# The refinement of the reciprocal rms moved from VectorE to GpSimd, and another order of the attention's events

## The chip, the cores and the metric

One core of a Trainium2 chip runs the whole kernel. Its engines work side by side, each through its own list of instructions in order: PE (TensorE, matrix products; PEld is its weight load), DVE (VectorE), ACT (ScalarE), POOL (GpSimd) and SP (SyncE, which here issues the DMA requests). The metric is the device time of one launch in microseconds (us); lower is better.

## What is computed

The reference, cut to what matters: attention with a normalisation by the root of the mean square on q and k, then a soft mixture of experts, then a two-layer network.

```
def rmsnorm(x, g):
    rms = np.sqrt(np.mean(x * x, axis=-1, keepdims=True) + 1e-06)
    return x / rms * g
# q, k, v: 4 batches, 12 heads, 448 rows, 64 columns
q_n, k_n = (rmsnorm(q, g_q), rmsnorm(k, g_k))
scores = q_n @ k_n.T / 8
attn = np.exp(scores - max) / (sum + 1e-9)
attn_out = attn @ v                       # 1792 x 768 over all heads
# soft mixture of 8 experts, 4 slots each, w1 768 x 1024, w2 1024 x 768
logits = x @ phi;  d = softmax over rows;  c = softmax over slots
slot_out = relu((d.T @ x) @ w1) @ w2;  x = c @ slot_out
# network, w_in 768 x 2048, w_out 2048 x 768
h = x @ w_in;  g = max(h, 0) + alpha * min(h, 0);  out = g @ w_out
```

## The kernel before

**Tiling.** The attention runs over 24 pairs of heads (4 batches times 6). Two pairs are one group for loading and for the normalisation, so there are 12 groups; pairs 2g and 2g+1 belong to group g. The 896 rows of a pair (two heads of 448) are cut into seven chunks of 128 rows. For every pair and chunk there is a product for the row maximum (`rowmax_mm`, PE; `rowmax`, VectorE), a score product (`score_mm`, PE), two exponentials (`score`, ACT), the difference between the f32 and the f16 exponential (`score_lo`, on GpSimd for chunks 3 and 6, on VectorE for others, on none for two) and a product with v (`av`, PE). After the attention the expert weights stream through (lines 1285 and 1314), and then the network runs (lines 1392 to 1521).

**The normalisation.** For each pair ACT squares q and k (line 641) and VectorE sums the squares into `u` (line 643), 28 columns for a group: two tensors, two pairs, seven chunks. `norm_rs` then makes `y`, the reciprocal of the rms: ACT takes Ln and Exp (lines 653 and 654), and one Newton step refines the result, y * (1.5 - u' * y * y) with u' half the mean square and the epsilon (lines 656 to 663). GpSimd multiplies q by y, k by the gains and then by y (`split_mul`, line 684), ACT casts to f16 (line 690), GpSimd subtracts to get the low part (`split_lo`, line 697), and PE transposes both (line 710). ACT copies the result out of PSUM (line 717), and SP issues small copies inside SBUF: `turned` (lines 719 and 721) and `twin`, which copies q to the other half of the partitions (line 726).

**The order.** Nothing of the attention is scheduled while it runs: the instructions of every engine are issued in the order in which the program was written out. The program first collects 2374 events in a list `plan`, always the same way (lines 1084 to 1140), and then sorts it by a tuple of literal positions, `ORDER`:

```
        assert sorted(ORDER) == list(range(len(plan)))
        plan = [plan[i] for i in ORDER]
```

`norm_rs` is cut into five events by its `yield`s: Ln and Exp; the scaling of `u`; nothing; y * y; the last two instructions. GpSimd's queue holds `split_mul`, `split_lo`, its `score_lo`, a little of the experts' sums, and it executes them in that order. SP's queue holds every request in the same way; a request that waits holds up those behind it. Weight loads are events of this list too, first in small pieces (`adv_pf`); when the last pair's scores are done, `close_score` frees buffers and all the loads that fit are issued in one go.

Of the kernel before, what the change touches and what calls it, by code (L numbers as in the profile page):

```python
# [16 lines left out]
ALU = mybir.AluOpType  # L17
# [336 lines left out]
def fused_attention_softmoe_mlp(  # L354
# [292 lines left out]
    def norm_rs(g):  # L647
# [5 lines left out]
        nc.scalar.activation(y, u, AF.Ln, scale=1.0 / D, bias=eps)  # L653
        nc.scalar.activation(y, y, AF.Exp, scale=-0.5)
        yield
        nc.vector.tensor_scalar(out=u, in0=u, scalar1=-0.5 / D, scalar2=-0.5e-6, op0=ALU.mult, op1=ALU.add)
        yield
        yield
        nc.vector.tensor_mul(t, y, y)
# [891 lines left out]
```

## Time and profile before

| | us |
|---|---|
| median of 3 runs | 698.97 |
| lowest and highest run | 695.72, 707.88 |
| the profiled execution | 698.2 |
| its span in the trace | 696.2 |

The span is the time from the first to the last recorded instruction. Busy times are sums over an engine's instructions; the chain that ended last is followed back from the last instruction, at each step to what released it. An engine's idle time is put down to the event that ended it. Times on GpSimd are rougher than on the other engines.

### The profile page before, as it was taken

The page shows a single profiled execution, that of the slowest core. Times are in us where ns is not written, and L with a number is a line of the kernel's source. Part 1 is how long each engine was busy: PE and PEld are TensorE (multiplying, and loading weights), DVE is VectorE, ACT ScalarE, POOL GpSimd, SP SyncE. Part 2 cuts the span into 40 slices and gives each one's busy share as a digit, 9 for nine tenths or more (in the row PEclk, how much of TensorE's full clock was granted, in tenths as well). Part 3 has the DMA queues.
Part 4 walks back from the last instruction along what each step waited for, and adds up shares of the span by engine and source line. Part 5 has one row for each costly group of instructions (what it writes and reads, how often), then busy time and mean ns, then how long its engine had stood idle before and what let it go on. Part 6 is the DMA issues. An engine that isn't in the chain of part 4 may idle for free.

```text
span 696.2 us, 14030 instructions
## 1 busy us (share of the span) xinstructions
PE 618.2 (89%) x5522; PEld 479.6 (69%) x5522; DVE 472.7 (68%) x967; ACT 364.5 (52%) x708; POOL 192.6 (28%) x200
## 2 busy tenths in 40 slices
PE   0799898898889999998998657899999999999997
PEld 0367665576656766775543213787899999999997
DVE  5788997899999999864311042999975545454541
ACT  2799996898898997772111121766531111111110
POOL 5976665466647654321101000000000000000000
PEclk9889999999999999998899979999999999999999
DMA  5477666644735622759799999250020101010101
GB/s 138 109 209 197 174 161 190 178 118 115 191 93 154 180 50 61 211 164 399 313 422 425 425 423 425 107 182 1 1 91 0 47 1 46 1 45 1 47 1 45
DMA packets 65425, 106.90 MB, mean 154 GB/s; under 512 B 34632, under 2 KB 51536, under 8 KB 61008
## 3 DMA queue, kind: packets, MB, share of 16 engines
q1 hardware_dynamic: 65360, 106.01, 45.6%
q8 instruction: 43, 0.70, 0.4%
q14 instruction: 22, 0.18, 0.1%
HBM read 92.18 MB, written 5.51 MB: 140 GB/s over the span
## 4 chain that ended last, share of the span: by engine, by line
PE 50%; DVE 23%; DMA 12%; ACT 8%; issue 3%; SPq 2%; POOL 2%; ACTq 0%; DVEq 0%; POOLq 0%
PE psa L1461 9%; PE psa L1460 9%; PE psa L1459 9%; DMA unit<-in_moe_w_dram 8%; DVE m L769 4%; PE psn L778 4%; PE psv L837 3%; PE psv L827 3%; PE psa L1285 2%; DVE e L810 2%; PE psr L760 2%; DVE wf L510 1%; ACT e L794 1%; PE psa L1314 1%; PE pst L1416 1%
## 5 line engine op out<-in xcount | busy, mean ns | idle before, releaser
L1459 PE MATMUL psa<-whi,gh 128*128 128x384 f32 (+1 forms) x448 | 152.7, 341 | 0.0
L1460 PE MATMUL psa<-wlo,gh 128*128 128x384 f32 (+1 forms) x448 | 151.8, 339 | 0.0
L1461 PE MATMUL psa<-whi,gl 128*128 128x384 f32 (+1 forms) x448 | 151.4, 338 | 0.0
L769 DVE TENSOR_REDUCE m<-psr 128x1 f16<-128x448 f32 x168 | 97.2, 615 | 5.9 <-PE psr L760 5.4
L1428 ACT CAST gh<-t 128x512 fp32r<-128x512 f32 x40 | 24.9, 622 | 123.0 <-DVE t L1425 122.5
L1461 PEld LDWEIGHTS psa<-whi,gl 128*128 128x128 f32 x448 | 84.7, 189 | 3.0 <-DVE gl L1408 0.2
L1460 PEld LDWEIGHTS psa<-wlo,gh 128*128 128x128 f32 x448 | 84.7, 189 | 2.8
L837 PE MATMUL psv<-vH,e 128*128 128x65 f16 (+1 forms) x1152 | 85.7, 195 | 1.0 <-DVE e L810 0.9
L1459 PEld LDWEIGHTS psa<-whi,gh 128*128 128x128 f32 x448 | 84.7, 189 | 2.6
L837 PEld LDWEIGHTS <-e 128*128 128x128 f16 (+1 forms) x1728 | 80.8, 106 | 1.5 <-DVE e L810 1.2
L1422 DVE TENSOR_SCALAR t<-pst,alpha_t 128x256 f32<-128x256 f32 x80 | 34.9, 476 | 61.9 <-PE pst L1416 61.9
L810 POOL TENSOR_TENSOR e<-ef,e 128x448 f16<-128x448 f32 x48 | 53.7, 1119 | 83.1 <-ACT ef L799 65.4
L827 PEld LDWEIGHTS psv<-vR,e 128*128 128x128 f32 (+1 forms) x384 | 59.6, 178 | 22.9 <-issue 10.9
L837 PE MATMUL psv<-vL,e 128*128 128x64 f16 (+1 forms) x576 | 73.7, 193 | 0.1
L794 ACT ACTIVATE e<-psn 128x448 f16<-128x448 f32 x120 | 65.1, 542 | 14.2 <-PE psn L778 11.1
L778 PE MATMUL psn<-q,k 128*128 128x448 f16 (+1 forms) x192 | 62.5, 368 | 11.0 <-DVE e L810 4.9
L827 PE MATMUL psv<-vR,e 128*128 128x65 f32 (+1 forms) x384 | 69.9, 264 | 1.9 <-DVE X L865 0.7
L760 PE MATMUL psr<-k,q 128*128 128x448 f16 (+1 forms) x192 | 58.8, 378 | 6.8 <-DVE m L769 4.0
L778 PE MATMUL psn<-qB,kB 67*128 67x448 f16 (+1 forms) x192 | 62.2, 364 | 2.8 <-DMA vR<-in_v_dram 2.8
L697 POOL TENSOR_TENSOR sp<-nf,sp 128x448 f16<-128x448 f32 x48 | 51.2, 1076 | 13.9 <-ACT sp L690 11.0
L810 DVE TENSOR_TENSOR e<-psn,e 128x448 f16<-128x448 f32 x72 | 44.2, 616 | 9.3 <-ACT psn L799 8.8
L710 PE MATMUL pst<-ident,sp 128*128 128x128 f16 x336 | 28.4, 233 | 19.2 <-POOL sp L697 19.0
(164 smaller groups left out, 1077.4 us busy)
## 6 DMA issues: line engine op xcount, KB each, us to landing
unit<-in_moe_w_dram SPq DMA_DIRECT2D x26, 1536.0 KB
unit<-in_moe_w_in_dram SPq DMA_DIRECT2D x24, 512.0 KB
rawo<-in_moe_w_out_dram SPq DMA_DIRECT2D x8, 1536.0 KB
unit<-in_moe_w_dram SPq DMA_DIRECT2D x36, 256.0 KB
out_dram<-osb SPq DMA_DIRECT2D x14, 384.0 KB
qk<-in_q_dram SPq DMA_DIRECT2D x24, 192.0 KB
qk<-in_k_dram SPq DMA_DIRECT2D x24, 192.0 KB
vR<-in_v_dram SPq DMA_DIRECT2D x48, 96.0 KB
```

The source lines that it names most:

```text
L697: eng.tensor_tensor(out=d["sp"][:, a, :, D:], in0=d["nf"][:, a], in1=d["sp"][:, a, :, 0:D], op=ALU.subtract)
L760: nc.tensor.matmul(pn[o0:o1, :S], d["q"][:, c0 : c0 + o1 - o0], d["k"][:, h * S : (h + 1) * S], start=True, stop=True)
L769: nc.vector.tensor_reduce(out=d["m"][:, c : c + 1], in_=d.pop(("pn", c))[:, :S], axis=AX.X, op=ALU.max)
L778: nc.tensor.matmul(pe[o0:o1, :S], lhs[:, c0 : c0 + o1 - o0], rhs[:, h * S : (h + 1) * S], start=st_, stop=not st_,)
L794: nc.scalar.activation(e2[:, 0], pe[:, :S], AF.Exp, scale=0.125)
L810: eng.tensor_tensor(out=e2[:, 1], in0=ef, in1=e2[:, 0], op=ALU.subtract)
L827: nc.tensor.matmul(pv[o0:o1, slot, :], d["e", c][:, qs], d["vv"][:, sl], start=(j == 0), stop=False,)
L837: nc.tensor.matmul(pv[o0:o1, slot, 0:wd], d["e", c][:, w // 2, qs], (vl if w == 1 else vh)[:, sl, 0:wd], start=(j == 0 and w == 0), stop=( ...
L1422: nc.vector.tensor_scalar(out=t0[:, cs], in0=ph[:, cs], scalar1=0.0, scalar2=alpha_t[:, f // 2, i : i + 1], op0=ALU.min, op1=ALU.mult)
L1459: nc.tensor.matmul(a, gh[f][:, ms], hi[:, hs], start=(f == 0 and not (packed and m % 2 == 1 and hf == 0)), stop=False)
L1460: nc.tensor.matmul(a, gh[f][:, ms], lo[:, hs], start=False, stop=False)
L1461: nc.tensor.matmul(a, gl[f][:, ms], hi[:, hs], start=False, stop=(f == KF - 1 and not (packed and m % 2 == 0 and hf == 1)))
```

## The change

The four instructions of the Newton step go from VectorE to GpSimd. The last of them, which on VectorE adds 1.5 and multiplies by y at once, becomes two, so that GpSimd gets five. The `yield`s, and with them the list of events, stay as they were. The tuple `ORDER` is a different permutation of the same 2374 positions; its first lines stand for the rest. The table of tuning values `T` is not changed.

```diff
@@ -230,123 +230,123 @@
 
 
 ORDER = (
-    1775, 968, 992, 1076, 920, 969, 993, 1016, 932, 1028, 1040, 1052, 1064, 1100, 1148, 1124, 921, 1796, 970, 994,
-    1172, 1797, 971, 995, 1196, 1244, 1220, 1077, 1101, 840, 850, 860, 870, 880, 890, 1268, 900, 910, 944, 1292, 1316,
...
+    1775, 921, 920, 1076, 968, 932, 992, 969, 993, 1016, 1028, 1040, 1052, 1064, 1100, 1148, 970, 1124, 1196, 1244,
+    1172, 994, 1796, 1220, 1077, 971, 2171, 1268, 1101, 840, 995, 1986, 1125, 850, 860, 870, 880, 890, 1292, 900, 910,
...
 )
@@ -653,14 +653,15 @@
         nc.scalar.activation(y, u, AF.Ln, scale=1.0 / D, bias=eps)
         nc.scalar.activation(y, y, AF.Exp, scale=-0.5)
         yield
-        nc.vector.tensor_scalar(out=u, in0=u, scalar1=-0.5 / D, scalar2=-0.5e-6, op0=ALU.mult, op1=ALU.add)
-        yield
-        yield
-        nc.vector.tensor_mul(t, y, y)
-        yield
-        nc.vector.tensor_mul(t, t, u)
-        yield
-        nc.vector.scalar_tensor_tensor(out=y, in0=t, scalar=1.5, in1=y, op0=ALU.add, op1=ALU.mult)
+        nc.gpsimd.tensor_scalar(out=u, in0=u, scalar1=-0.5 / D, scalar2=-0.5e-6, op0=ALU.mult, op1=ALU.add)
+        yield
+        yield
+        nc.gpsimd.tensor_tensor(out=t, in0=y, in1=y, op=ALU.mult)
+        yield
+        nc.gpsimd.tensor_tensor(out=t, in0=t, in1=u, op=ALU.mult)
+        yield
+        nc.gpsimd.tensor_scalar(out=t, in0=t, scalar1=1.0, scalar2=1.5, op0=ALU.mult, op1=ALU.add)
+        nc.gpsimd.tensor_tensor(out=y, in0=t, in1=y, op=ALU.mult)
         y4 = y.rearrange("p (a i c) -> p a i c", a=2, i=GP)
         for gi in range(GP):
             st[g * GP + gi]["y"] = y4[:, :, gi]
```

Some places that the two tuples give to the same event, in steps (the number of row-maximum and score products before it in the program, halved; seven steps are one pair, 168 the whole attention):

| event | before | after |
|---|---|---|
| `twin` of pair 18 ahead of its first score | 4.0 | 1.0 |
| `twin` of pair 20 ahead of its first score | 4.5 | 0.5 |
| last q/k request of pairs 10 and 11 ahead of the square | 7.0 | 4.0 |
| last q/k request of pairs 16 and 17 ahead of the square | 4.0 | 6.0 |
| last q/k request of pairs 18 and 19 ahead of the square | 5.5 | 2.5 |
| `norm_rs` of group 11, first and last event | 133.0, 136.0 | 133.5, 136.5 |
| `close_norm` | 163.0 | 158.5 |

## Rows read from the trace of the kernel before

**Rows 1.** The page: the span, and each engine's busy time.
```profile
span 696.2 us, 14030 instructions
...
PE 618.2 (89%) x5522; PEld 479.6 (69%) x5522; DVE 472.7 (68%) x967; ACT 364.5 (52%) x708; POOL 192.6 (28%) x200
```

**Rows 2.** Busy time by stage: stretch, length, engines; PE clock, DMA share, GB/s.
```profile
15.00:30.00 15.00, 9.00 (x51) 4.72 (x52) 8.68 (x17) 9.51 (x16) 14.02 (x15) 0.98 0.44 109
...
60.00:270.00 210.00, 188.73 (x2390) 138.84 (x2388) 200.59 (x412) 186.50 (x379) 128.09 (x120) 0.98 0.54 145
...
305.00:430.00 125.00, 100.89 (x890) 48.91 (x891) 33.16 (x101) 27.23 (x54) 10.41 (x18) 0.92 0.97 397
```

**Rows 3.** Timeline of SP's requests: start, length, engine, line, request.
```profile
303.85 17.59 SPq L479 DMA_DIRECT2D unit<-in_moe_w_dram  x17
```

**Rows 4.** Lines 656 to 663: shortest/median/longest in ns, first and last start.
```profile
L656 DVE TENSOR_SCALAR u<-u x12: 163/172/706, 14.0 to 255.5; 128x28 f32<-128x28 f32 x12
...
L659 DVE TENSOR_TENSOR t<-y x12: 173/178/186, 14.3 to 255.6; 128x28 f32<-128x28 f32 x12
...
L661 DVE TENSOR_TENSOR t<-t,u x12: 177/186/190, 14.5 to 257.8; 128x28 f32<-128x28 f32 x12
...
L663 DVE SCALAR_TENSOR_TENSOR y<-t,y x12: 186/187/1029, 14.7 to 258.0; 128x28 f32<-128x28 f32 x12
```

**Rows 5.** The chain that ended last, in order of time: start, length, what.
```profile
17.91 1.04 POOL sp L697
...
27.62 1.00 POOL sp L697
...
76.39 0.08 DVE u L656
...
76.82 0.81 DVE y L663
...
214.64 0.19 DVE y L663
...
219.38 2.57 DMA q<-q
```

**Rows 6.** GpSimd's small products by line and shape: busy us, mean ns, idle before.
```profile
L1211 POOL TENSOR_TENSOR cs<-cN,cs 128x128 f32<-128x128 f32 x8 | 3.5, 458 | 33.0 <-DVE cs L1210 33.0
...
L1151 POOL TENSOR_TENSOR G<-gqk 128x64 f32<-128x64 f32 x1 | 0.3, 317 | 4.3 <-DMA gqk<-in_g_k_dram 4.3
```

**Rows 7.** Timelines of ACT and POOL: start, length, operation; in brackets the idle time.
```profile
14.03 0.23 ACT L654 ACTIVATE y<-y 128x28 f32<-128x28 f32 x1
...
15.00 0.93 POOL L684 TENSOR_TENSOR nf<-qk,y 128x448 f32<-128x448 f32 x1 [2.16 <-DVE y L663]
...
25.79 0.94 POOL L684 TENSOR_TENSOR nf<-qk,y 128x448 f32<-128x448 f32 x1 [0.65 <-DVE y L663]
...
29.68 1.13 POOL L684 TENSOR_TENSOR nf<-qk,G 128x448 f32<-128x448 f32 x1
30.89 0.94 POOL L684 TENSOR_TENSOR nf<-nf,y 128x448 f32<-128x448 f32 x1
...
251.29 0.23 ACT L654 ACTIVATE y<-y 128x28 f32<-128x28 f32 x1
...
258.25 1.40 POOL L684 TENSOR_TENSOR nf<-qk,y 128x448 f32<-128x448 f32 x1 [4.52 <-DVE y L663]
```

**Rows 8.** Waits (total us, times, longest): whole span; ACT, 30:310; PE's loads, 60:310.
```profile
POOL nf L684 <- DVE y L663: 24.1, 9, 5.2
...
ACT sqr L641 <- DMA qk<-in_k_dram: 2.0, 1, 2.0
...
PEld L710 <- POOL sp L697: 0.9, 2, 0.5
```

**Rows 9.** One VectorE line in the attention, and the same after 335 us.
```profile
L510 DVE SCALAR_TENSOR_TENSOR win<-unit,win 128x768 uint32<-128x768 uint32 x16 | 17.1, 1067 | 0.3
...
L510 DVE SCALAR_TENSOR_TENSOR wf<-rawo,wf 128x768 uint32<-128x768 uint32 x16 | 15.2, 951 | 0.0
```

230 rows, old and new, of the table ORDER are left out of this document.

## The prediction

> **What bounds the kernel now.** I read the page first. [rows 1] gives the span, 696.2 us, and the engines' shares of it: PE 89%, DVE 68%, ACT 52%, POOL (GpSimd) 28%. These are means over stages with different limits, so the next view is the table by stage [rows 2]. From 15 to 30 us GpSimd is busy for 14.0 of 15 us: its normalisation paces the start. From 60 to 270 us, the dense part of the attention, VectorE is busy for 200.6 of 210 us (96%), PE for 188.7 (90%), ACT for 186.5 (89%) and GpSimd for 128.1 (61%). From 305 to 430 us the DMA engines are 97% busy: the expert weights stream in. The change touches the attention alone, so VectorE in the dense part is the engine to look at.
>
> Does a gain in the attention reach the end? The weight stream begins with a burst of 17 requests at 303.85 us [rows 3], issued once the last pair's scores are done. A shorter attention issues it earlier, and the stream, whose length is set by bytes, ends earlier by as much. So a microsecond of attention counts as a microsecond of the end.
>
> **What is taken from VectorE.** Twelve times, once for two pairs, `norm_rs` issues four instructions on 28 columns there [rows 4]. At the medians a group is 0.172 + 0.178 + 0.186 + 0.187 = 0.72 us, twelve are 8.7 us; the two longest (0.706 and 1.029) add 0.53 and 0.84: 10.1 us of VectorE's 472.7 [rows 1]. That isn't what the end gets. Eight of the groups lie between 60 and 270 us, among them the longest instruction: 8 x 0.72 + 0.84 = 6.6 us, if VectorE bounded every moment of that stage. This is the upper bound. The lower bound is the chain that ended last: between 76 and 215 us these lines stand in it with 13 pieces in four of the groups, 2.6 us together, of which 0.81 is the longest [rows 5]. VectorE is 96% busy there, but only some of its work is on the chain; I take the middle, **-4.6 us**.
>
> **What is put on GpSimd.** Five instructions a group; the fused last one becomes two. The trace has no such instructions on GpSimd, so their price is bounded by rows. Below: what VectorE takes, 0.17 us [rows 4]. Above: GpSimd's product on 64 columns, 0.317 [rows 6]. On 128 columns it takes 0.458, so a column is (0.458 - 0.317) / 64 = 2.2 ns and 28 columns are 0.317 - 36 x 0.0022 = 0.24 us, which I take. Each step reads the one before: at 30.89 us such a reader starts 0.08 us after its predecessor's end at 29.68 + 1.13 [rows 7]. A group is 5 x 0.24 + 4 x 0.08 = 1.5 us (bounds 0.9 and 1.9), twelve are 18 us. In the dense part 8 x 1.5 = 12 us take GpSimd from 61% to 67%.
>
> There it is covered. GpSimd stood 24.1 us in nine waits for just this `y` [rows 8], which VectorE got to late: in the last group Exp ended at 251.29 + 0.23 = 251.5 us, and the multiply by y began, after 4.52 us of waiting, at 258.25 [rows 7]. The change puts a wait for ACT's Ln and Exp into GpSimd's own queue. Behind it stand the multiplies by y, the f16 low parts of q and k and the score differences of chunks 3 and 6, and for those wait ACT's cast, PE's transposes and PE's products with v. Between 60 and 310 us PE's weight loads stood 0.9 us for GpSimd's low parts [rows 8], and in the list of waits of that stretch no product with v waits for GpSimd. So I cost the dense part at nothing; without that cover it costs the 12 us.
>
> At the start there is no cover: the chain runs through GpSimd with little pause from 17.91 to 28.62 us [rows 5]. Group 0: Exp ends at 14.26 us and the multiply by y starts at 15.00 [rows 7]. On GpSimd the first step is done beside Exp, and four remain: 4 x 0.24 + 3 x 0.08 = 1.2, so 15.5: +0.5 us. Group 1: 1.5 us come into a busy queue, and the wait of 0.65 us for y, ended at 25.79, goes: +0.9. Group 2 comes after 35 us, past this stretch. Of these 1.4 us later pairs may regain some, as ACT's work on them overlaps; from 0 to 1.4, I take **+1.1 us**.
>
> **Sharing between VectorE and GpSimd.** One weight-narrowing line of 768 columns takes 1.067 us while GpSimd works and 0.951 later, when it is idle [rows 9]: 16 x 0.116 = 1.9 us lost. GpSimd's added work is about a tenth of its work in that stretch, so 0.2 us more here; VectorE's other operations between SBUF operands may lose as much again: **+0.5 us** (0 to 3).
>
> The Trainium skill (SBUF — State Buffer, section "SBUF: two separate sides") says that VectorE operations with two SBUF inputs share a port pair with GpSimd as an exclusive lock, the loser fully blocked. The trace agrees that such a line is slower, by 0.116 us [rows 9].
>
> **The order.** I decoded both tuples with the plan's own construction. 450 of 624 PE events change place, by 1.7 places in the mean and 14 at most; GpSimd's least. Leads are measured in steps: one step is one row-maximum product and one score product, 168 in all over the 290 us from 15 to 305, so 1.7 us each. Better: q and k of pairs 16 and 17, for which ACT once waited 2.0 us [rows 8], are requested 6.0 steps before use instead of 4.0. Worse: the copy of q to the other half (`twin`) comes 1.0 and 0.5 steps before pairs 18 and 20 are scored, where it had 4.0 and 4.5. One such copy stood on the chain for 2.57 us [rows 5]; at leads of 1.7 and 0.9 us the two could hold PE for 0.9 + 1.7 = 2.6 us. The requests for pairs 10 and 18 lose 3 steps, but keep 4.0 and 2.5. Two us gained and 2.6 lost, both on paper: I take 0, with 3 us to either side. SP's requests are the same in number and size. `close_norm` stands 4.5 steps earlier and could start two weight loads sooner; as all cut loads are issued before the burst at 303.85 in both orders: nothing.
>
> **Sum.** -4.6 + 1.1 + 0.5 + 0 = -3.0 us on the profiled execution's 698.2 us (span 696.2 and 2.0 around it): 695.2. The median of the runs, 698.97, is 0.8 above that execution, and the three spread from 695.7 to 707.9; the forecast is **695.5**, by itself 692 to 698.
>
> **The rivals.**
> 1. Relief that doesn't arrive. PE and ACT are 90% and 89% busy in the dense part; if they fill whatever VectorE leaves, only the charges stay: 698.97 + 1.6 = 700.5, or 698 with a part of the relief. The 13 pieces of the chain speak against it.
> 2. All of it arrives and the order gains: 698.97 - 6.6 + 1.6 - 3 = 691, and 687 if GpSimd's earlier y, 4 to 5 us in the late groups, shortens the way of the last pairs too. VectorE's 96% speaks for it; that eight groups aren't on the chain, against.
> 3. The slower side: GpSimd becomes the late one. Each group puts 1.5 us of small steps ahead of score differences that PE needs, and it decides once these land after PE reaches their product with v. If half of the dense groups pay in full, with the chain's relief alone: 698.97 + 6 + 1.6 - 2.6 = 704; with all of them 710. Against it speak GpSimd's 61% and the 24.1 us of waits that go.
>
> The Trainium skill (GPSIMD Engine Reference, section "Engine selection") speaks for rival 3: elementwise work belongs on VectorE, and GpSimd is about twice as slow with two inputs. At twice 0.19 us five steps would be an estimated 1.9 us a group, the upper end of what the rows gave.
>
> 4. The short leads of the order cost their 3 us and the relief is only the chain's: 698.97 - 2.6 + 1.6 + 3 = 701 (699 to 702).
>
> **How the numbers follow.** Forecast 0.50 (692 to 698), rival 1 0.17 (698 to 700.5), rival 2 0.13 (687 to 692), rival 4 0.10 (699 to 702), rival 3 0.10 (702 to 711). Without rival 3 and the lowest part of rival 2 this is 688 to 702, some 0.85 of the chance. Two per cent, about what a measurement of this kernel can tell from no change, is 685.0 to 713.0. No case centres outside it; its tails get faster 0.04 and slower 0.04, and within is 0.92.
>
> **What would show it.** Right: VectorE's four lines gone; five on GpSimd of 0.2 to 0.3 us; no wait of GpSimd for VectorE's y; PE's first products about half a us later; the burst of 17 requests some 3 us before 303.85 and all after it shifted by as much. Wrong: VectorE's share falls and the burst stays (rival 1); PE's products with v wait for GpSimd (rival 3); PE waits for q's copy in pairs 18 and 20 (rival 4); GpSimd's small steps take 0.5 us or more, or an unseen cost comes with them.

## The result, and the profile after

| | before | after |
|---|---|---|
| median of 20 runs each, side by side on one chip, us | 695.64 | 699.89 |
| lowest and highest | 692.67, 707.88 | 696.48, 705.23 |
| ratio after to before, 95% interval | | 1.0063 [1.0040, 1.0086] |
| the profiled execution and its span | 698.2, 696.2 | 700.74, 699.0 |

The change makes the kernel 0.6% slower, 4.4 us. The prediction said 3.0 us faster. 699.89 lies outside the 692 to 698 that it gave the forecast, inside the 688 to 702 that it gave with its rivals, and on the other side of no change. The forecast stood on the three runs of before at hand then, with a median of 698.97; the twenty here have 695.64, so that the absolute 695.5 looks nearer than the forecast change was. Line numbers of after are one higher from the last refinement step on (L664 is that step; L685 `split_mul`, L727 `twin`, L739 the copy of the row maxima, L779 the score product).

The page of after, span and busy times, against [rows 1], and the dense part against [rows 2] (length, then PE, PE loads, DVE, ACT, POOL, PE clock, DMA share, GB/s):

```profile
span 699.0 us, 14051 instructions
...
PE 620.8 (89%) x5522; PEld 480.9 (69%) x5522; DVE 466.8 (67%) x919; ACT 364.2 (52%) x708; POOL 212.8 (30%) x260
...
60.00:270.00 210.00, 191.02 (x2441) 141.15 (x2439) 202.34 (x394) 191.25 (x391) 145.65 (x165) 0.99 0.55 149
```

The 48 instructions are gone from VectorE and 60 are new on GpSimd. VectorE's busy time falls by 5.9 us, not by the 10.1 that the durations of the 48 add up to; GpSimd's grows by 20.2. In the same 210 us every engine does more than before, GpSimd 17.6 us and the others 1.8 to 4.8. The stretches from the start to 285 and to 320 us, before first, then after, show where the loss stands:

```profile
0.00:285.00 285.00, 240.06 (x2882) 171.88 (x2882) 256.78 (x543) 239.30 (x482) 176.10 (x177) 0.96 0.55 147
0.00:320.00 320.00, 274.46 (x3391) 198.98 (x3392) 279.79 (x601) 263.81 (x534) 185.43 (x186) 0.97 0.56 154
```

```profile
0.00:285.00 285.00, 240.89 (x2950) 174.29 (x2950) 255.77 (x507) 244.60 (x493) 198.33 (x239) 0.99 0.56 151
0.00:320.00 320.00, 272.32 (x3383) 198.86 (x3384) 273.77 (x551) 263.56 (x534) 205.58 (x246) 0.98 0.56 154
```

At 285 us PE has executed 68 instructions more in after (2950 against 2882), at 320 us 8 fewer: this execution was ahead and lost its lead in the last 35 us. SP's requests there (start, length, engine, line, request), after first, then a kernel that is the same but for one event (experiment 3):

```profile
292.24 5.83 SPq L479 DMA_DIRECT2D unit<-in_moe_w_dram  x11
298.41 0.50 SPq L727 DMA_DIRECT2D q<-q  x1
299.05 0.49 SPq L479 DMA_DIRECT2D unit<-in_moe_w_dram  x1
299.78 0.79 SPq L739 DMA_DIRECT2D qB<-mr  x1
314.80 6.96 SPq L479 DMA_DIRECT2D unit<-in_moe_w_dram  x5
```

```profile
298.92 0.50 SPq L730 DMA_DIRECT2D q<-q  x1
302.48 0.76 SPq L742 DMA_DIRECT2D qB<-mr  x1
303.34 16.08 SPq L482 DMA_DIRECT2D unit<-in_moe_w_dram  x17
```

In after, eleven weight pieces of 256 KB go out at 292.24, ahead of the last pair's small copies of q and of the row maxima. In the other kernel, as in the kernel before [rows 3], they go out in the burst behind these copies. After's chain that ended last, its waits between 295 and 312 us, and two stretches by engine show what that does; the last line is one of these stretches in experiment 3's trace:

```profile
293.60 4.74 DMA unit<-in_moe_w_dram
...
298.41 7.05 DMA q<-q
...
305.50 1.67 PE psn L779 x4
```

```profile
PEld L779 <- DMA q<-q: 3.4, 1, 3.4
PE psn L779 <- DMA q<-q: 3.3, 1, 3.3
```

```profile
300.00:305.00 5.00, 1.99 (x20) 1.27 (x18) 2.05 (x7) 1.87 (x4) 1.14 (x2) 0.95 0.77 247
305.00:310.00 5.00, 4.50 (x33) 3.59 (x34) 0.62 (x1) 2.32 (x5) 0.00 (x0) 0.50 0.02 5
```

```profile
305.00:310.00 5.00, 4.88 (x78) 4.22 (x77) 1.89 (x4) 3.51 (x8) 1.03 (x1) 1.00 0.98 318
```

The copy of q overwrites half of a tile that the pair's row-maximum products still read. The last of these starts at 295.07 and takes 0.35 us, so the copy could be requested at 295.42; its request comes at 298.41, 3.0 us later, when SP has issued the eleven pieces (292.24 + 5.83 = 298.07). In before and in experiment 3 the request comes within 0.05 us of that product's end. The copy itself, 112 KB, then takes 7.05 us; a copy like it took 2.57 on the chain of before [rows 5]. PE is busy for 1.99 of the 5 us from 300, and in the next 5 us its granted clock is 0.50, the lower of its two levels (1.2 GHz). In the traces of before and of experiment 3 PE waits for no transfer between 295 and 312 us, and its clock there is 1.00. From 305 to 315 the DMA engines have almost nothing to do (share 0.02 and 0.01): the five whole loads that are left wait for the last pair's scores and go out at 314.80 (before, 314.38). So the pieces came 11.6 us sooner than before's burst, and the stream's last part no sooner.

GpSimd's refinement of group 0 (timeline; start, length, operation), and what is left of GpSimd's waits for y (whole span: total, times, longest):

```profile
14.09 0.21 POOL L656 TENSOR_SCALAR u<-u 128x28 f32<-128x28 f32 x1 [0.34 <-ACT y L653]
14.38 0.23 POOL L659 TENSOR_TENSOR t<-y 128x28 f32<-128x28 f32 x1
14.69 0.24 POOL L661 TENSOR_TENSOR t<-t,u 128x28 f32<-128x28 f32 x1
15.03 0.21 POOL L663 TENSOR_SCALAR t<-t 128x28 f32<-128x28 f32 x1
15.32 0.24 POOL L664 TENSOR_TENSOR y<-t,y 128x28 f32<-128x28 f32 x1
15.64 0.93 POOL L685 TENSOR_TENSOR nf<-qk,y 128x448 f32<-128x448 f32 x1
```

```profile
POOL u L656 <- ACT y L653: 10.2, 6, 6.0
```

A group takes 15.64 - 14.09 = 1.55 us, and the 24.1 us of waits for VectorE's y [rows 8] have become 10.2 us for ACT's.

### The profile page after: what moved, and what is told of

It reads as the page before. It is cut to its first block, busy times and chain, and to the rows that moved or that the text cites. A ratio compares the mean times of both kernels' runs of the same rounds, so it can differ in the third digit from the quotient of the medians.

```text
span 699.0 us, 14051 instructions
## 1 busy us (share of the span) xinstructions
PE 620.8 (89%) x5522; PEld 480.9 (69%) x5522; DVE 466.8 (67%) x919; ACT 364.2 (52%) x708; POOL 212.8 (30%) x260
## 4 chain that ended last, share of the span: by engine, by line
PE 47%; DVE 24%; DMA 14%; ACT 6%; issue 4%; POOL 3%; SPq 2%; POOLq 0%; DVEq 0%; ACTq 0%
DMA unit<-in_moe_w_dram 9%; PE psa L1462 9%; PE psa L1461 9%; PE psa L1460 9%; DVE m L770 4%; PE psn L779 3%; PE psv L838 3%; PE psa L1286 2%; PE psv L828 2%; DVE e L811 2%; DMA q<-q 2%; POOL nf L685 2%; DVE win L514 1%; DVE wf L510 1%; PE psa L1315 1%
## 5 line engine op out<-in xcount | busy, mean ns | idle before, releaser
L811 POOL TENSOR_TENSOR e<-ef,e 128x448 f16<-128x448 f32 x48 | 55.7, 1160 | 76.4 <-ACT ef L800 62.4
L828 PEld LDWEIGHTS psv<-vR,e 128*128 128x128 f32 (+1 forms) x384 | 61.4, 180 | 24.2 <-issue 10.8
L779 PE MATMUL psn<-q,k 128*128 128x448 f16 (+1 forms) x192 | 62.1, 369 | 12.4 <-DVE e L811 5.4
L779 PE MATMUL psn<-qB,kB 67*128 67x448 f16 (+1 forms) x192 | 62.0, 367 | 0.5 <-DMA qB<-mr 0.5
L1286 PE MATMUL psa<-unit,slT 128*32 128x512 f32 x192 | 36.3, 717 | 10.2 <-DMA unit<-in_moe_w_dram 9.4
```

What stands on the lines that cost most here:

```text
L779: nc.tensor.matmul(pe[o0:o1, :S], lhs[:, c0 : c0 + o1 - o0], rhs[:, h * S : (h + 1) * S], start=st_, stop=not st_,)
L811: eng.tensor_tensor(out=e2[:, 1], in0=ef, in1=e2[:, 0], op=ALU.subtract)
L828: nc.tensor.matmul(pv[o0:o1, slot, :], d["e", c][:, qs], d["vv"][:, sl], start=(j == 0), stop=False,)
L1286: nc.tensor.matmul(ph[hf][32 * g : 32 * g + 32, :], slT[:, t, :], wu[:, t % 3, hf * 512 : (hf + 1) * 512], start=(hf, g) not in seen, stop ...
```

## The experiments

All ratios are to the kernel before, run beside each kernel on the same chip (its median there was 695 to 697), with a 95% interval; two kernels from different chips are compared by their ratios.

**1 and 2. Which half of the change costs?** The move alone under the order of before, and the order alone with the refinement on VectorE.

```diff
 # 1: after, with before's tuple
-ORDER = (1775, 921, 920, 1076, ...
+ORDER = (1775, 968, 992, 1076, ...
 # 2: before, with after's tuple
-ORDER = (1775, 968, 992, 1076, ...
+ORDER = (1775, 921, 920, 1076, ...
```

> The refinement on GpSimd as in the changed kernel, the order of events as before. Theory A (the move itself pays and the new order's late part loses it): the attention's tail is undisturbed, and the time is 2 to 5 us below before, ratio 0.993 to 0.997. Theory B (the 5 us by which the changed kernel leads near 300 us come from the new order, not from the move): same as before or up to 2 us slower, ratio 1.000 to 1.003. Rival C (the move itself is the loss, GpSimd being late): 4 us or more slower, ratio 1.006 and above.

> The new order of events with the refinement left on VectorE. Theory A: the stall before the last pair's scores stays and the relief is missing, so it is slower than the changed kernel: ratio to before 1.010 to 1.015. Theory B: the order alone makes both the lead and the stall, so the time is that of the changed kernel, ratio 1.004 to 1.008. Rival C: faster than the changed kernel, ratio near 1.000.

Measured: the move alone 700.69, ratio 1.0078 [1.0040, 1.0116]; the order alone 716.66, 1.0272 [1.0224, 1.0320]. Each half by itself is slower, and the two together (1.0063) are far from the 3.5% that they add up to. So the two are not separate terms of a sum.

**3 and 4. The earlier `close_norm`.** One event moved, in either direction: in after it goes behind the last pair's two copies; in before, ahead of them by ten pieces.

```diff
 # 3: after's ORDER
-..., close_norm, <11 pieces of weights>, ..., twin(23), ..., turned_m(23), ...
+..., <11 pieces, now waiting for close_norm>, ..., twin(23), ..., turned_m(23), close_norm, ...
 # 4: before's ORDER
-..., score_lo(21, 3), ..., twin(23), ..., turned_m(23), close_norm, ...
+..., score_lo(21, 3), close_norm, ..., twin(23), ..., turned_m(23), ...
```

> The changed kernel with one event moved: close_norm, which opens the buffers for two more weight loads, stands after the last pair's row of maxima is sent (as before the change) instead of ahead of the last pair's copy of q. Theory (the weight pieces ahead of that copy in SP's queue and in the DMA engines hold PE): the copy lands in about 2 to 3 us instead of 7, PE's wait of 3 to 4 us and the low clock after it go, and the time falls by 5 to 8 us below the changed kernel, ratio to before 0.993 to 0.999. Rival (the copy's short lead, or the scores' order, is what holds PE): no more than 2 us gained, ratio 1.003 to 1.006.

> The kernel before with the same event moved the other way: close_norm ahead of the last pair's copy of q, with ten weight pieces between. Theory: the copy waits behind the pieces, PE stalls before the last pair's scores, 5 to 8 us slower than before, ratio 1.007 to 1.012. Rival: the old order leaves enough work between to hide it, ratio 0.999 to 1.002.

Measured: 3 gives 696.61, 0.9993 [0.9965, 1.0021]; 4 gives 700.65, 1.0054 [1.0018, 1.0090]. The place of this one event is worth 0.70% in after (1.0063 to 0.9993, 4.9 us; the two medians are 3.3 us apart, but the kernels before beside them differ by 1.2 us) and 0.54%, 3.8 us, in before. This is shown in both directions. In the trace of 4 the copy of q takes 6.73 us, PE waits 1.5 us for it, and its granted clock from 305 to 310 us is 0.66.

**12. SP's queue, or the transfers?** After, with the last pair's two copies issued on ACT's queue; the pieces stay early (from 295.25 us in its trace).

```diff
-        nc.sync.dma_start(t[D:], t[:D])
+        (nc.scalar if n == NP_ - 1 else nc.sync).dma_start(t[D:], t[:D])
-        nc.sync.dma_start(qB[n % NKB][D : D + 1], mr)
+        (nc.scalar if n == NP_ - 1 else nc.sync).dma_start(qB[n % NKB][D : D + 1], mr)
```

> The changed kernel with the last pair's two small copies (q to the other half, and the row maxima) issued on ACT's own DMA queue instead of SP's, close_norm left where the change put it. If standing behind eleven weight pieces in SP's queue is what delayed them: the delay of 7 us goes while the weight stream keeps its earlier start, so at or below the kernel before, 692 to 696, ratio 0.995 to 1.001. If the pieces that already occupy the DMA engines delay them in any queue: as the changed kernel, 698 to 700, ratio 1.003 to 1.007.

Measured: 699.73, 1.0066 [1.0034, 1.0098], as the changed kernel. The request (timeline of ACT) and the copy on the chain:

```profile
299.35 0.56 ACTq L727 DMA_DIRECT2D q<-q  x1
...
299.35 7.51 DMA q<-q
```

The copy no longer waits for SP: its request comes 0.9 us after the last row-maximum product of its pair (298.08 + 0.35), behind some of ACT's exponentials, where in after it came 3.0 us behind. It still takes 7.51 us. So its place in SP's queue was a part of the delay in after, some 2.1 us of it; the larger part, 7.51 against 2.57 us, is the copy's own time beside the pieces (DMA share 1.00 from 300 to 305 us). The Trainium skill (DMA: Bandwidth & Descriptors, section "Issuing engines are not separate DMA queues") says that requests of any engine end on the same 16 DMA engines and interleave; the 7.51 us here beside the 7.05 on SP's queue agree. PE waits 1.4 us for this copy, in after 3.3, its clock from 305 to 310 us is 1.00, and the time is after's all the same. The three kernels with early pieces lose 0.54 to 0.66%, though PE waits 3.3, 1.5 and 1.4 us for the copy and the clock falls to 0.50, to 0.66 and not at all. So the price of the event's place is shown, but not that all of it goes through this wait and this clock; ACT's queue also pays for the two requests here (0.56 and 1.32 us).

**5, 6 and 11. The relief alone, the charge alone, nothing.** All three under before's order. 5 leaves the refinement out of the computation; 6 keeps it on VectorE and adds GpSimd's five steps on scratch tiles; 11 only has the two scratch tiles.

```diff
 # 5
-        nc.vector.tensor_scalar(out=u, ...)   # and the other three
 # 6, beside VectorE's four
+        nc.gpsimd.tensor_scalar(out=sA, in0=sA, scalar1=1.0, scalar2=0.0, ...)
+        nc.gpsimd.tensor_tensor(out=sB, in0=sA, in1=sA, op=ALU.mult)
...
 # 6 and 11
+    sA = ac.tile([P, 28], F32, name="sA")
+    sB = ac.tile([P, 28], F32, name="sB")
```

> The kernel before, in its own order, with the refinement left out (y is what Exp gives): VectorE loses its 48 small instructions and GpSimd gets nothing. This prices the relief alone. Theory A (relief is worth what the chain and the busy time said): 2.6 to 6.6 us below before, ratio 0.990 to 0.997. Theory B (VectorE's relief is filled by PE and ACT, so the move had nothing to win): same as before, ratio 0.998 to 1.002.

> The kernel before, in its own order and with its refinement on VectorE, and five more small steps per group on GpSimd at the same places, on scratch data (60 instructions more, no new wait). This prices the charge on GpSimd alone, without its wait for Ln and Exp. Theory A (only the start has no cover): 1 to 2 us above before, ratio 1.001 to 1.003. Theory B (the steps delay what PE needs all through the attention): 5 us and more, ratio 1.006 and above.

> The kernel before with two more scratch tiles of 28 columns, set once at the start and never used: tiles behind them move by 224 bytes a partition, nothing else changes. Theories 'load' and 'early y': 695 to 697, ratio 0.999 to 1.001. Theory 'anything costs': 698 to 700, ratio 1.004 to 1.007, and then the losses of all runs under the old order are no statement on VectorE and GpSimd.

Measured: 5 699.78, 1.0065 [1.0030, 1.0099]; 6 699.61, 1.0050 [1.0011, 1.0089]; 11 696.87, 1.0016 [0.9988, 1.0044]. An edit that does nothing shows no difference. The charge on GpSimd costs some 0.5%, but its interval overlaps that of 11, which has the same tiles. And the relief by itself, with nothing put anywhere, is a loss of 0.65%: the prediction's largest term has the wrong sign under this order.

**9 and 10. Is it the load, or the earlier y?** Both leave the refinement out of the computation. 9 puts four VectorE instructions on scratch in its place: the load is back, y stays early. 10 keeps one VectorE instruction on y: y is late, three quarters of the load are gone.

```diff
 # 9, in the place of the four steps
+        nc.vector.tensor_scalar(out=sA, in0=sA, scalar1=1.0, scalar2=0.0, ...)
+        nc.vector.tensor_mul(sB, sA, sA)
+        nc.vector.tensor_mul(sB, sB, sA)
+        nc.vector.scalar_tensor_tensor(out=sA, in0=sB, scalar=0.0, in1=sA, ...)
 # 10, in the place of the fourth step
+        nc.vector.tensor_scalar(out=y, in0=y, scalar1=1.0, scalar2=0.0, ...)
```

> The kernel before, its refinement left out of the computation as in the run without it, but with four VectorE instructions of the same kinds and 28 columns on scratch tiles in its place: VectorE's load is that of before, and y is ready straight from ACT. Theory 'load' (the written order is fitted to the time that VectorE's four steps take, so taking them out is what cost 0.65%): the load is back, so 695 to 697, a ratio of 0.999 to 1.002. Theory 'early y' (y's earlier arrival changes when GpSimd and ACT run their work): as without the refinement, 699 to 700, ratio 1.004 to 1.008. Theory 'anything costs' (any neutral edit moves the time that much): 698 to 700 too, told apart by the run with the scratch tiles alone.

> The kernel before with the first three steps of the refinement left out of the computation; the fourth stands as one VectorE instruction that multiplies y by 1 at the same place of the order, so y is handed on by VectorE as late as before, and three quarters of the load are gone. Theory 'load': most of the loss of the run without the refinement, 698 to 700, ratio 1.003 to 1.007. Theory 'early y': no loss, or the relief of up to three quarters of the forecast 4.6 us: 692 to 696, ratio 0.995 to 1.001.

Measured: 9 710.32, 1.0209 [1.0171, 1.0246]; 10 696.72, 1.0028 [0.9992, 1.0064]. Neither loss nor gain can be told in 10, so relief without an earlier y brings nothing that can be seen. 9 is worse than either theory had it. Its trace shows one reason: the small steps now run while GpSimd works, where before GpSimd stood still for most of them (by shape, 60 to 270 us: busy us, mean ns, idle before):

```profile
L659 DVE TENSOR_SCALAR sA<-sA 128x28 f32<-128x28 f32 x8 | 3.0, 375 | 0.0
...
L666 DVE SCALAR_TENSOR_TENSOR sA<-sB,sA 128x28 f32<-128x28 f32 x7 | 3.5, 498 | 0.2
```

The same operations had medians of 172 and 187 ns in before [rows 4] (means of 185 and 292 in this stretch). One step at 77.98 us, with GpSimd idle, takes 0.17 us; one at 107.73, beside a GpSimd product from 107.58 to 108.62, takes 0.92. The 48 steps take 20.7 us in all, where before's took 10.2 in the same view. GpSimd's wait for y was a quiet time for VectorE's steps; with an early y they meet its work. How much of the 2.1% this makes isn't shown.

The narrowing lines, the 64 instructions of [rows 9]'s kind, show it too. Here are those of before and of 5 (by shape, 15 to 320 us):

```profile
L769 DVE TENSOR_REDUCE m<-psr 128x1 f16<-128x448 f32 x168 | 97.2, 615 | 5.9 <-PE psr L760 5.4
L514 DVE SCALAR_TENSOR_TENSOR win<-unit,win 128x768 uint32<-128x768 uint32 x16 | 16.4, 1025 | 0.2
L504 DVE TENSOR_SCALAR win<-win 128x768 f32<-128x768 f32 x16 | 8.9, 559 | 0.0
L506 DVE TENSOR_SCALAR win<-win 128x768 uint32<-128x768 uint32 x16 | 8.9, 558 | 0.4
```

```profile
L764 DVE TENSOR_REDUCE m<-psr 128x1 f16<-128x448 f32 x168 | 97.3, 616 | 8.4 <-PE psr L755 7.9
L514 DVE SCALAR_TENSOR_TENSOR win<-unit,win 128x768 uint32<-128x768 uint32 x16 | 19.0, 1190 | 0.2
L510 DVE SCALAR_TENSOR_TENSOR win<-unit,win 128x768 uint32<-128x768 uint32 x16 | 16.2, 1010 | 0.3
L504 DVE TENSOR_SCALAR win<-win 128x768 f32<-128x768 f32 x16 | 10.4, 650 | 0.0
L506 DVE TENSOR_SCALAR win<-win 128x768 uint32<-128x768 uint32 x16 | 10.0, 626 | 0.4
```

The 64 take 17.1 + 16.4 + 8.9 + 8.9 = 51.3 us in before and 55.6 in 5, though L510 alone falls from 17.1 to 16.2; the row maxima, which read PSUM, stay at 0.615 us. The Trainium skill (SBUF — State Buffer, section "SBUF: two separate sides") says that the contention lies on the port pair that VectorE shares with GpSimd, and not for VectorE's other ports; the lines on SBUF that grow and the PSUM line that doesn't agree with it.

**7 and 8. The start.** Groups 0 and 1 back on VectorE, the others on GpSimd: 7 under before's order, 8 under that of experiment 3.

```diff
+        if g < 2:
+            nc.vector.tensor_scalar(out=u, ...)   # the four steps
+        else:
             nc.gpsimd.tensor_scalar(out=u, ...)   # the five steps
```

> The order of before, the refinement on VectorE for the first two groups and on GpSimd for the other ten. Theory A (the move's loss in the old order lies in the first 30 us, where GpSimd sets the pace): the loss goes and some relief remains, 693 to 696, ratio 0.995 to 1.000. Theory B (the loss lies in the dense part, where small steps and the wait for Exp hold GpSimd's queue): it stays, ratio 1.004 to 1.008.

> The changed kernel with close_norm late, as in the run before, and the refinement of the first two groups on VectorE. Theory A (start and late part are its two losses): faster than before by 2 to 4 us, ratio 0.993 to 0.998. Theory B (the new order fits the steps on GpSimd at the start, and VectorE's come late there): same as the run with close_norm late alone or slower, ratio 0.999 to 1.006.

Measured: 7 702.98, 1.0127 [1.0079, 1.0175]; 8 697.25, 1.0017 [0.9990, 1.0044]. Taking the charge from the start gains nothing in either order (1 had 1.0078, 3 had 0.9993). So the 0.64 and 1.5 us by which the first two groups come later in after aren't seen at the end; the prediction's bound of 0 was the better value.

**13 and 14. The same question inside the new order.** The order of experiment 3, with the refinement left out of the computation (13), and on VectorE (14).

```diff
 # 13: experiment 5's norm_rs, 14: before's norm_rs, both with
+ORDER = (<after's tuple, close_norm behind turned_m(23)>)
```

> The changed kernel's order with close_norm behind the last pair's copies, and the refinement left out of the computation (y straight from ACT's Exp): neither VectorE nor GpSimd has its steps. Theory 'relief is worth something, GpSimd's charge takes it back': below the same order with the steps on GpSimd (696.6), by 3 to 6 us: 690 to 694, ratio 0.991 to 0.997. Theory 'VectorE's lines pay for an early y, and what is left of the relief ends in waits for PE': 695 to 701, ratio 0.999 to 1.008, with the 64 narrowing instructions of the attention nearer the 55.6 us of the old order without the refinement than the 52.2 us of the changed kernel.

> The changed kernel's order with close_norm behind the last pair's copies, and the refinement on VectorE as before. Theory 'each order is fitted to where the refinement runs': still 1.5 to 2.3% slower than the kernel before, 706 to 711, since the early close was worth 0.7% of the 2.7% that the new order lost with VectorE. Theory 'most of that loss was the early close': 696 to 700, ratio 1.001 to 1.007.

Measured: 13 692.95, 0.9961 [0.9930, 0.9992]; 14 713.24, 1.0231 [1.0176, 1.0286]. With 1, 3 and 5 the table is full:

| refinement | order of before | new order, `close_norm` late |
|---|---|---|
| on VectorE | 1 | 1.0231 |
| on GpSimd | 1.0078 | 0.9993 |
| left out | 1.0065 | 0.9961 |

In the new order the move is worth 2.4%, and in the old one it costs 0.8%. 13's 64 narrowing instructions take 18.9 + 17.9 + 10.9 + 8.8 = 56.5 us, more than in 5, and it is still the fastest of all. So the longer VectorE lines are there, but they don't decide: my theory of experiments 9 and 10 falls as the cause of the loss under the old order. 14 has long waits in GpSimd's queue (timeline):

```profile
61.93 0.94 POOL L687 TENSOR_TENSOR nf<-qk,y 128x448 f32<-128x448 f32 x1 [3.19 <-DVE y L666]
...
267.94 0.94 POOL L687 TENSOR_TENSOR nf<-qk,y 128x448 f32<-128x448 f32 x1 [6.11 <-DVE y L666]
```

The new tuple puts the first multiply by y closer behind the last refinement step: counted in score products between the two, groups 3 to 7 and 9 had leads of 1, 4, 1, 1, 2 and 3, and now have 0, 3, 0, 0, 1 and 0. On GpSimd a lead of 0 brings no wait for another engine; with VectorE between, GpSimd waits up to 6.11 us (5.2 in before [rows 8]). But all its waits for y are 19.6 us, seven of them, less than before's 24.1 us in nine, so their sum doesn't explain the loss. What stands behind them does grow: between 30 and 305 us ACT's casts wait 7.8 us for GpSimd's products (1.9 in before, 1.4 in 3). How much of 14's 2.3% this makes isn't shown.

## Why the prediction was wrong, point by point

**The step that failed: `close_norm` at nothing.** The prediction saw that the event stands 4.5 steps earlier and asked only whether the loads gain. It argued that all cut loads go out before the burst in both orders. In the trace of before, twelve of the burst's seventeen requests are themselves cut pieces, and it is `close_norm` that lets them go. It didn't ask what the pieces are moved past: the last pair's copies, for which PE waits. The runs put 0.70% on the event's place in after, 4.9 us, and 3.8 us in before (experiments 3 and 4); the whole loss of after is 4.4. In after's trace the copy comes 3.0 us late in SP's queue and takes 7.05 us beside the pieces, and PE waits 3.3 us for it. Rival 4 had a late copy of q that stops PE, but at pairs 18 and 20 and from short leads; it came at pair 23, from the queue and the transfers. Without the early event the kernel is level with before, where the sum had -3.0 us: the rest of the miss is that the relief, less its charges, came to nothing.

**The relief, -4.6 us.** No run shows it. Under the order of before the relief alone costs 0.65% (5) or can't be seen (10); in the new order, leaving the whole refinement out gains 0.4%, 2.7 us, against before (13). Two things were mis-sized. The durations overlap: the busy times of VectorE's lines add up to 512.9 us in before, while the page counts 472.7 for the engine; without the 48 short ones it is 5.9 us less and not 10.1, of which 2.2 at most is the growth of its lines on SBUF (51.3 to 52.2 and, for line 747, 18.4 to 19.7). And a middle between "VectorE bounds everything" and "what stood on the chain" isn't an estimate of what the end gets where PE and ACT are 90% busy too. Rival 1, that PE and ACT fill what VectorE leaves, is nearest in kind, but the move alone costs 1.0078, which would be 698.97 + 5.5 where it had + 1.6. That 699.89 lies in its range (698 to 700.5), and in rival 4's, is in part luck: both stand on 698.97, and on the 695.64 of the twenty runs rival 1's sum is 697.2.

**GpSimd's price** was right: 1.5 us a group forecast, 1.55 measured; 18 us in all, 19.3 measured (GpSimd's whole busy time grows by 20.2), as some single steps take up to 1.02 us. Group 0's multiply by y came at 15.64 (15.5 forecast), group 1's at 27.29 instead of 25.79 [rows 7] (+0.9 forecast, +1.5 came). What it costs in the end was too small: +1.6 with the sharing, against 0.5% or 3.5 us in experiment 6, and 0.3% between 13 and 3; neither is clear of noise, since 6 overlaps with 11 and 13 with 3.

**The waits for y** went as forecast, and brought nothing: GpSimd's `score_lo` already stood 65.4 us for ACT between 15 and 320 us, and in experiment 5, where the waits for VectorE's y go, it stands 78.3 us. GpSimd was early for its next work anyway.

**The order at 0, with 3 us to either side.** Its own effect isn't a number: it is +2.3% with the refinement on VectorE and -0.8% with it on GpSimd (both with `close_norm` late, the latter against experiment 1). The prediction summed the move and the order as if each had a price by itself, and they have none.

**Rival 3**, GpSimd the late one in the dense part, didn't come: between 60 and 310 us PE's weight loads wait 0.4 us for GpSimd in after, 1.1 in before, and GpSimd is busy for 145.65 of 210 us.

**What stays open.** Why before's order loses 0.65% when the refinement is simply gone. Its narrowing lines grow by 4.3 us there, but they grow by 5.2 in 13, which gains. That a written order is fitted to the durations it was made with is what the table suggests; which waits carry it isn't shown, since single profiles differ too much: after and 12 are the same up to the last pair's copies, and the last row-maximum product starts at 295.07 in one and at 298.08 in the other. The changed kernel's 4.4 us are shown to hang on the early `close_norm`, since without it the kernel is level with before; by which waits beyond the one for q stays open (experiment 12). No version with the refinement in it beat the kernel before; 13, without it, is 0.4% faster.

## What to carry to other kernels

Where an edit lets a large transfer go earlier, look for the small copies that it is moved past, and ask what waits for those: here the stream's last part waited for the end of the stage, and an early first part gained nothing. Where the instruction order is written out, a move and the order that comes with it have no separate prices; run the two by two table before believing a sum. Busy time taken from the busiest engine need not be time saved while two others are 90% busy; sum short instructions by the page's busy time, not by their durations.

## What the hardware showed that was not expected

A 112 KB copy from SBUF to SBUF took 7.05 us behind eleven transfers of 256 KB, 6.73 and 7.51 in the other two kernels of that kind, on SP's queue or ACT's, and 2.57 where such a copy stood on the chain of before. Issuing the eleven took SP 5.83 us, 0.53 each, time that a request behind them waits. After PE had been busy for 1.99 of 5 us, its granted clock was 0.50 in the next 5. VectorE's 28-column steps took 375 to 498 ns in the mean when GpSimd had no wait for them (experiment 9), against means of 178 to 292 and medians of 172 to 187 in before (the two longest 0.71 and 1.03 us). On GpSimd the same steps took 213 to 244 ns in the median, 1.2 to 1.3 times VectorE's (means 268 to 383), with 0.29 to 0.34 us from start to start in group 0.
